# A chunked recurrence rebuilt as one fixed order of tasks, shorter placement lists, and 33 matmuls that nothing reads

## The chip, the cores and the metric

The kernel runs on one core of a Trainium2 chip. The metric is device time in microseconds (us) of one execution; three executions of the kernel before took 553.8, 552.11 and 552.08 us, the median being 552.11 us. The core has five engines with a queue of instructions each: TensorE (PE, whose weight loads are shown apart as PEld), VectorE (DVE), ScalarE (ACT), GpSimd (POOL) and SyncE (SP), which issues most of the DMA transfers. An engine carries out its own queue in order and waits on semaphores for what others make.

## The reference

Two parts follow one another. The first is a delta-rule recurrence over 768 time steps for 4 batches x 8 heads, with a 48x48 state each; the second sends each of the 3072 tokens (the 8 heads' outputs side by side, 384 numbers) to the best of 8 experts, a two-layer network with 1024 hidden units.

```python
k_n = k / (norm(k) + 1e-6)
for t in range(768):                         # state: 48 x 48 per batch and head
    y[t]  = q[t] @ state
    state = state + beta[t] * outer(k_n[t], v[t] - k_n[t] @ state)
x = y as 3072 rows of 384
logits = x @ w_gate + modality_bias[modality_id]
e = argmax(logits); gate = softmax(logits)[e]
out[tokens of e] = gate * (relu(x @ w1[e]) @ w2[e])
```

With this input only two experts are chosen, by 1508 and by 1564 tokens, so that the experts' work is five blocks ("slots") of 512 tokens, two of 256 and one of 128 in both kernels.

## The kernel before, in words

**Recurrence.** Time is cut into 12 chunks of 64 steps. A group step i = 2c+g (24 of them) treats chunk c for half of the 32 sequences. For each half step `gram` (L124) multiplies the keys with keys and queries: per sequence pair one stationary tile KB of 112x128, in which the keys of two sequences stand block-diagonally. KB is filled by copies (L111 to L113, the helper's L32 and L33) for each half step. The product gives the key Gram matrix and, beside it, the query-key matrix, which is masked to its lower triangle (L143 on DVE for the late half, on POOL in L145 for the early one).

From the Gram matrices come inverses of 32x32 triangular blocks. They are made for six sets m = 0..5, one after another, by `inverse_`: 30 pairs of a multiply (L213) and a subtract (L214), each pair for one column, on 128 partitions; rows 0 to 12 of each set go to DVE (tiles `tm_x`), the rest to POOL (`tm_y`). Set 0 is made in blocks of 16 which matmuls (L247, L253) join. `level` puts the blocks together to 64x64 for a group step (L326, a scaled copy `ys`, L335, a copy of R, and the scaling of the values in L340 on POOL).

`chain_` is the sequential part, one call per group step, each of which needs the state left by the step of the same g before it: L363 (ks, keys times state), a subtraction on DVE (L365, RHS), L378 (z, the inverse applied), a copy by ACT (ZT), L386 (state update into PSUM tile Sps), L372 and L394 (the output y), copies of the state (Sbd) and the output (xo), and a store of xo to DRAM (xd) by SP. `route` turns the outputs (L463) and multiplies them with the gate weights (L468, 128x96 wide).

**Routing.** `rank` finds each token's expert and its rank there. `lists` turns ranks into lists "place to token": for 6 tiles of 128 tokens at a time DVE makes a one-hot tile `l0` (L508) and two tiles `l1` with NH columns per token tile (L562 to L564), and PE multiplies them (L566). `part_a` treats the first 18 token tiles (four slots a0..a3 come from it), with NH = 16; `part_b` all 24 (slot b0, two of 256 and one of 128, and what is only needed by other inputs), with NH = 44.

**Experts.** Slots follow one another in the order a0, a1, a2, a3, b0, c0, c1, e0. A slot loads its expert's weights, gathers its tokens from xd (POOL), turns them (L659), splits weights (L674 high part on ACT; low part L675 on DVE, and on POOL for a1 and b0) and tokens (L661, L662) into high and low halves, and multiplies three times for each product: layer 1 in L690, followed by relu (L692, L693), layer 2 in L733, scaled by the gate (L736) and scattered to the output (L737). Slots of 128 tokens use L710.

**What sets the order.** The tile framework decides the order of each engine's queue from the program's order, priorities and a model of durations; the program sets a few priorities itself (`part_b` is under a raised one) and ties some instructions behind others. `tile_kernel` (L740) calls `gram`, `inverse`, `chain`, `route` and `level` in a loop (L777) and then runs the slots.

Of the kernel before, what the change touches and what calls it, by code (L numbers as in the profile page):

```python
# [14 lines left out]
class C:  # L15
    fl=4; mw=1; wn=2; kqb=5; kbb=2; thr=9; g0=17; nh=4; LA=2; LA0=1; ge=14; ge1=16; lgk={0:11,1:15,2:17,3:17}; gg={(12,0):('jy',0),(12,1):('jr',0),(13,0):('y1',0),(13,1):('r',0)}; ga=1; i1l=1; gdq=1;  gw=0; ww=512; t2e='vector'; dq1=('scalar','scalar'); jn={1:((1,0),)}; pf=0; gs=0
    invat={3:0,7:1,11:2,15:3,19:4,23:5}
    pgk=12; pgb=2; pgr=3; pg_q='sync'; gdb=2; kqr=2; kvb=2; r64=2; rtb=1; rcb=3; rbb=1; abuf=2; xob=2
    kb_q='sync'; gdfix='vector'; gdv=4; tmem='vector'; ascale='vector'; rscale='vector'; rcopy='mask'; rm_e='gpsimd'; vq='gpsimd'; yev='scalar'; sv=()
    x_q='sync'; xa_q='sync'; kv_q='sync'; ld_q='sync'; inv_q='sync'; w_q='sync'  # L20
    ap=(0,1); rp=(0,1); ra={0:('scalar','vector'),1:('scalar','vector')}; rs=(0,); i0=16; kb1=('scalar','vector'); g1=1; yq=2; na=1; xgb=4; wlp=('a1','b0'); wlq=(0,1,2,3); hpa=0; hpb=1; wide=1; zte=('scalar','scalar'); zti=4; pC_=None; pcn=(); gpt=('mo','ks','mo','y'); gpn=16; wte='vector'; ls=0; sp1=12; ti='gpsimd'; gde='scalar'; gde0='vector'; e16='scalar'; rh0='scalar'; as0='gpsimd'; dq=('vector','vector'); k1=1; rtg='gp'; rl=-1; fk=0; fz=0; fy=0; fi=0
    cA=9; tB=22; gt_e='gpsimd'; lb_e='vector'; TA=512; SB=1; SC=2; SE=1; eo=0; hold=1
    A1=2; A2=4; A3=1; B1=6; B2=6; B3=1
    lg0=1; hs=12; hn=10; tmb=2
    split=range(6); sp=3; spe=1
    invp=(); kbc=24; dkb=0
    la_e='vector'; rw=dict(reuse_waits='tile'); pC=0; pI=None; pL=None; pin=(0,); pln=(0,); kbp=4; kbe0=('scalar','scalar'); kbe=('vector','vector'); pml=range(0,16); sp0=1; r0=6; NR=10; kg=0; a0=1; wr=4; gl=16; SA=4; i1=60

NS=16; NE=8
# [5 lines left out]
def ring(pool,k,name,dt=F32):  # L35
    return pool.tile([128,1536],dt,name=name,tag=f"ring{k}")

class Attention:
    """Chunked delta rule. Group step i=2c+g: 64 tokens of chunk c of batches 2g+p, heads 4h+j; x=4p+j."""
    def __init__(s,ident,ctx,pctx,tc,kq,kv,bblk,mask,xd,pm):  # L40
        nc=s.nc=tc.nc; s.tc=tc; s.kq,s.kv,s.bblk,s.xd,s.pm=kq,kv,bblk,xd,pm
        s.ident=ident; s.late=[]
        for n in ("PG","KE","KQ","KV","Pt","GU","GD","gd","D","RD","RE","R","W","GW","AW","Y1","IL","RR","RL","RW","LD","rr","todo","KD","PI"): setattr(s,n,{})
        pc=s.pc=ctx.enter_context(tc.tile_pool(name="ac",bufs=1))
        s.pl=ctx.enter_context(tc.tile_pool(name="al",bufs=2))
        s.pw=ctx.enter_context(tc.tile_pool(name="aw",bufs=2))
# [12 lines left out]
    def rings(s):
        nc=s.nc; ring=s.ring; V=nc.vector; pc=s.pc  # L60
        s.Ic=pc.tile([128,1,16],F32,name="Ic"); s.m16=pc.tile([128,1],F32,name="m16")
        V.tensor_reduce(s.Ic[:,0],s.ident.rearrange("p (q r) -> p r q",q=4)[:,0:16],AX.X,ALU.add)
        V.tensor_reduce(s.m16,s.Ic[:,0],AX.X,ALU.add)
        V.tensor_scalar(s.m16,s.m16,-1.0,None,ALU.add)
        s.RHS=ring("RHS",2,[128,8,96],nc.gpsimd)
        s.R64=ring("R64",C.r64,[128,16,64],nc.gpsimd)
        s.RTB=ring("RTB",C.rtb,[128,16,64],nc.gpsimd)
        s.ZT=ring("ZT",2,[128,8,96],nc.gpsimd)
        s.Sbd=ring("Sbd",2,[112,8,96],nc.gpsimd)
    def banks(s,router):  # L70
        nc=s.nc; s.router=router
        bank=[s.ps.tile([128,512],F32,name=f"Sps{g}",tag=f"S{g}") for g in range(2)]
        for t in bank: nc.vector.memset(t,0.0)
        s.Sps=[t[0:112,0:384].rearrange("r (j c) -> r j c",j=4) for t in bank]
        router.lg=[t[:,384:480].rearrange("r (c e) -> r c e",e=8) for t in bank]

    def early(s,ctx):
        nc,tc=s.nc,s.tc
        s.pe=ctx[0].enter_context(s.tc.tile_pool(name="ag",bufs=1))
        s.pi=ctx[1].enter_context(s.tc.tile_pool(name="ai",bufs=1,side="right"))  # L80
        wt=s.wt=s.pe.tile([128,512],F32,name="wt")
        getattr(nc,C.wte).memset(wt,0.0)
        wz=s.pm.tile([128,512],F32,name="wz",tag="mo",bufs=2)
        for r in range(C.wn): nc.tensor.matmul(wz[:,0:C.ww],wt[:,0:128],wt[:,0:C.ww],start=True,stop=True)
        s.KB=[s.pe.tile([112,8,128],F32,name=f"KB{g}") for g in range(C.kbb)]
        for g,t in enumerate(s.KB): (s.nc.vector,s.nc.gpsimd)[g%2].memset(t,0.0)

    def gate(s,ins): return s.tc.issue_after(ins.ins) if ins is not None else contextlib.nullcontext()

    def fetch(s,i):  # L90
        c,g=divmod(i,2)
        if c<2:
            if g==0: s.KQ[c]=s.pl.tile([112,2,8,2,64],F32,name=f"kqr{c}",tag="kqr",bufs=C.kqr)
            s.KE[i]=k=s.KQ[c][:,g]
        else: s.KE[i]=k=s.pe.tile([112,8,2,64],F32,name=f"ke{i}",tag="ke",bufs=C.kqb)
        w=None
        if c>=2: w=s.LD[C.kg] if i>=C.g0 and C.kg>=0 else s.GW.get(c-C.thr)
        with s.gate(w): s.KD[i]=getattr(s.nc,C.ld_q).dma_start(k,s.kq[c].rearrange("r (g x a t) -> r g x a t",g=2,x=8,a=2)[:,g])

    def gram(s,i):  # L100
        nc,tc=s.nc,s.tc; E=lambda n:getattr(nc,n)
        c,g=divmod(i,2); m,n=divmod(i,4)
        if g==0:
            s.PG[c]=ring(s.pr,c%C.NR,f"PG{c}")
            if m not in C.ap: s.gd[c]=s.pe.tile([128,2,2,4,32],F32,name=f"gd{c}",tag="gd",bufs=C.gdb)
        if n==0:
# [4 lines left out]
        for h in range(2):  # L111
            b=64*h
# [746 lines left out]
```

## Time and profile before

| | us |
|---|---|
| median of three runs | 552.11 |
| span of the profiled execution | 550.4 |
| start of the first expert matmul (L690, slot a0) | 295.64 |
| start of the first L690 of slot a1 | 352.87 |
| end of the last L733 | 540.05 |

The profile is of one execution. Its page gives busy time per engine, the span in slices, the DMA queues, a chain of waits followed back from the last instruction, and the costliest groups of instructions. In a row of a group, "L213 DVE TENSOR_TENSOR tm_x<-T,A 128x108 ... x165 | 57.8, 352 | 5.4 <-DVE PG L143 0.7" stands for: line 213 on DVE, tile tm_x made from T and A, 165 instructions, 57.8 us busy in total and 352 ns in the mean, and 5.4 us idle ahead of them, most of which ended when the named instruction did. A row of a timeline has the start, the busy time, and the instruction, with "x16" for 16 like records in a row (one fp32 matmul leaves two records). A table by stretches has for each engine the busy time and the number of records, then PEclk, the TensorE clock that was granted as a share of full speed, the busy share of the DMA engines and their GB/s. A busy TensorE at a low granted clock does less work in the same time.

### The profile page before, as it was taken

How to read it: one execution, taken by the hardware profiler on the slowest of the kernel's cores; microseconds unless marked ns; L12 is line 12 of the kernel's file. 1: busy time of each engine (PE TensorE's matmuls, PEld its weight loads, DVE VectorE, ACT ScalarE, POOL GpSimd, SP SyncE). 2: the span in 40 equal slices, each digit the busy share in tenths (PEclk: the TensorE clock that was granted, in tenths of full speed). 3: DMA queues.
4: the chain of work that ended last, by engine and by line, in shares of the span. 5: the costliest groups of instructions: out<-in, count | busy, mean ns of one | idle time of the engine just before them, and what ended most of it. 6: DMA issues, size and time to landing. Idle time of an engine off the chain costs nothing. (4 is left out here: it accounts for less than half of the span.)

```text
span 550.4 us, 14025 instructions
## 1 busy us (share of the span) xinstructions
PE 483.5 (88%) x5459; PEld 432.1 (79%) x5459; DVE 364.5 (66%) x877; ACT 263.5 (48%) x619; POOL 208.5 (38%) x350
## 2 busy tenths in 40 slices
PE   7876875897898897998889997799999999999992
PEld 5776865786687776787768896689889898899992
DVE  5999899998789689577474499435536233437850
ACT  6855631655766567476565403043424334216540
POOL 9863477065066263111142136242303437111110
PEclk9977796588899799798889998699999999999997
DMA  8979741233594975838864224233623524427720
GB/s 205 247 200 238 176 105 55 64 95 89 169 226 138 236 180 166 209 120 230 228 192 142 76 80 127 75 116 114 209 79 120 170 75 164 128 78 227 233 85 9
DMA packets 82716, 80.81 MB, mean 147 GB/s; under 512 B 50105, under 2 KB 73671, under 8 KB 81520
## 3 DMA queue, kind: packets, MB, share of 16 engines
q1 hardware_dynamic: 79440, 70.18, 46.8%
q0 software_dynamic: 3200, 9.64, 5.2%
q8 instruction: 45, 0.74, 0.6%
q14 instruction: 31, 0.25, 0.2%
HBM read 65.12 MB, written 14.88 MB: 145 GB/s over the span
## 5 line engine op out<-in xcount | busy, mean ns | idle before, releaser
L733 PE MATMUL opa<-w2ha,h 128*128 128x384 f32 x256 | 69.1, 339 | 0.3 <-DVE ooa L736 0.3
L213 DVE TENSOR_TENSOR tm_x<-T,A 128x108 f32<-128x108 f32 (+12 forms) x165 | 57.8, 352 | 5.4 <-DVE PG L143 0.7
L124 PE MATMUL gp<-ke,KB 112*128 112x128 f32 x320 | 53.1, 331 | 9.3 <-DVE PG L143 3.9
L214 DVE TENSOR_TENSOR T<-T,tm_x 128x108 f32<-128x108 f32 (+12 forms) x165 | 56.8, 346 | 4.5
L124 PEld LDWEIGHTS gp<-ke,KB 112*128 112x128 f32 x320 | 48.3, 238 | 12.3 <-issue 3.7
L693 DVE SCALAR_TENSOR_TENSOR h<-hpa,h 128x512 fp32r<-128x512 f32 x32 | 22.0, 689 | 42.4 <-ACT h L692 42.4
L733 PEld LDWEIGHTS opa<-w2ha,h 128*128 128x128 f32 x256 | 46.2, 188 | 1.4 <-DVE ooa L736 0.5
L733 PE MATMUL opa<-w2la,h 128*128 128x384 f32 x128 | 43.0, 336 | 0.0
L692 ACT ACTIVATE h<-hpa 128x512 fp32r<-128x512 f32 x32 | 19.1, 596 | 49.5 <-PE hpa L690 49.5
L690 PE MATMUL hpa<-x,w1ha 128*128 128x512 f32 x144 | 39.1, 408 | 0.0
L340 POOL TENSOR_TENSOR kvn<-kvn,RR 128x384 f32<-128x384 f32 x22 | 18.7, 868 | 50.7 <-DMA kvn<-in_kv_dram 28.3
L363 PE MATMUL ks<-Sbd,kqr 112*64 112x96 f32 x352 | 27.3, 274 | 8.7 <-DMA kqr<-in_kq_dram 4.8
L365 DVE TENSOR_TENSOR RHS<-kvn,ks 64x384 f32<-64x384 f32 x44 | 24.2, 551 | 15.8 <-POOL kvn L340 9.4
L214 POOL TENSOR_TENSOR T<-T,tm_y 128x18 f32<-128x18 f32 (+8 forms) x90 | 30.7, 342 | 6.6
L213 POOL TENSOR_TENSOR tm_y<-T,A 128x18 f32<-128x18 f32 (+8 forms) x90 | 30.5, 339 | 6.6
L690 PEld LDWEIGHTS hpa<-x,w1ha 128*128 128x128 f32 x144 | 27.3, 194 | 5.5
L32 ACT COPY ZT<-z 64x384 f32<-64x384 f32 x48 | 22.7, 473 | 17.2 <-PE z L378 16.6
L363 PEld LDWEIGHTS ks<-Sbd,kqr 112*64 112x64 f32 x352 | 20.9, 150 | 11.8 <-ACT Sbd L32 4.4
L32 ACT COPY Sbd<-Sps 48x192 f32<-48x192 f32 x88 | 27.5, 313 | 5.2 <-PE Sps L386 2.7
L737 POOL DMA_INDIRECT out_dram<-ooa,sidxa x16 | 17.1, 1071 | 32.6 <-DMA out_dram<-ooa,sidxa 13.1
L657 POOL DMA_INDIRECT xga<-xd,gidxa x16 | 17.9, 1117 | 30.5 <-PE xpa L659 17.4
L378 PE MATMUL z<-RHS,R 128*64 128x96 f32 x384 | 26.9, 296 | 1.6 <-ACT R L338 1.6
(346 smaller groups left out, 1173.7 us busy)
## 6 DMA issues: line engine op xcount, KB each, us to landing
kvn<-in_kv_dram SPq DMA_DIRECT2D x12, 768.0 KB, 8.0
ke<-in_kq_dram SPq DMA_DIRECT2D x20, 448.0 KB, 6.8
kqr<-in_kq_dram SPq DMA_DIRECT2D x10, 896.0 KB, 6.9
w1ra<-in_moe_w_dram SPq DMA_DIRECT2D x16, 384.0 KB, 4.0
w2ra<-in_moe_w_dram SPq DMA_DIRECT2D x16, 384.0 KB, 3.2
xd<-xo SPq DMA_DIRECT2D x24, 192.0 KB, 2.5
w1rc<-in_moe_w_dram SPq DMA_DIRECT2D x8, 384.0 KB, 3.6
w2rc<-in_moe_w_dram SPq DMA_DIRECT2D x8, 384.0 KB, 3.2
```

Of the source, the lines that this page charges most:

```text
L32: if n=="scalar": nc.scalar.copy(o,i)
L124: nc.tensor.matmul(gp[p][:,j,:],KB[:,x,:],k[:,x].rearrange("r a t -> r (a t)"),start=True,stop=True)
L213: yield I.tensor_tensor(o,y,z,ALU.mult)
L214: yield I.tensor_tensor(x,x,o,ALU.subtract)
L340: if c: E(C.vq).tensor_tensor(V,V,w,ALU.mult)
L363: nc.tensor.matmul(ks[64*p:64*p+64,:,j,:],KQ[:,4*p+j,0],hc(Sb[:,4*p+j,:]),start=True,stop=True)
L365: b=64*p; nc.vector.tensor_tensor(RH[b:b+64,:,48*p:48*p+48].rearrange("q (h j) c -> q h j c",h=2),VN[b:b+64],ks[b:b+64],ALU.subtract)
L378: s.PI['z',i]=nc.tensor.matmul(z[64*h:64*h+64,:,j,:],R[:,2*j+h,:],hc(RH[:,4*h+j,:]),start=True,stop=True)
L690: nc.tensor.matmul(hp[:,v,:],w[:,k,fs],x[:,k,0:T],start=(n==0),stop=(n==8)); n+=1
L692: nc.scalar.activation(hh,hp,AF.Relu)
L693: nc.vector.scalar_tensor_tensor(hl,hp,0.0,hh.bitcast(F32),ALU.max,ALU.subtract)
L733: mm=nc.tensor.matmul(op,h[:,f%nf,ts_],w[:,f%2,:],start=(n==0),stop=(n==23)); n+=1
```

## The change

The recurrence is written as about 916 named tasks (load, gram, copy, one pair of an inverse, one product of a step, ...), each with the tasks that it needs. A string of their numbers, `ORDER`, gives the one order in which they are emitted; a letter behind a number puts the task on another engine than its usual one (d DVE, a ACT, g POOL). `in_order` then chains the instructions of each engine, so that they keep this order. Also new:

- Gram matrices without KB: for each chunk 32 matmuls of 64x64 for keys with keys and, as a task of its own, 32 for queries with keys. The copies into KB go, and the mask is always applied by DVE.
- Inverses for two sets in one instruction, JOBS = ((0,1),(2,3),(4,5)): sets 0 and 1 as 16-blocks with joins on the chip, the others with two sets side by side. 27 of 60 pairs of these stand on POOL, the rest on DVE.
- Gate logits for four token tiles together (12 matmuls of 32x128 instead of 3 of 128x96 for each tile).
- The routing of the first 16 token tiles (8 columns, two slots a0, a1), and slot a0's loads, gathers, token turning and its first four of eight layer-1 parts are tasks in the same order; the slots are now a0, a1, b0, b1, b2, c0, c1, e0.
- `part_b` makes 17 columns instead of 44, for 4 tiles at a time; the remaining 35 are made only in the branch for other inputs, which this input does not take in either kernel.
- Ten matmuls of the identity at the start (`WARM`) in place of two of 512 columns, and 33 of them at 16 places of the order (`FILL`) into a part of a PSUM tile that nothing reads.
- All low halves of weights are made on DVE (`wlp` is empty).

```diff
+JOBS=((0,1),(2,3),(4,5)); SPL=(0, 32, 32)
+NS=16; NE=8; NC=24; WARM=10
+ORDER="""\
+167 42 2 0 26 54 161 58 56 43 55 57 65 44d 46d 59 47a 68d 66 27 69a 162 36 67 75 45 53 48 76 28 70 159 79 3 64 80 1 77 29 163 78 81 86 4 87 160 164 165 88 89 90 49 337 166 30 338
...
+FILL="""\
+444:3 82:1 150:6 857:2 382:1 869:1 725:1 492:3 867:1 806:1 632:2 511:4 521:1 554:2 357:3 559:1"""
...
+    def order(s):
+        out=[]; done=set()
+        for n in ORDER.split():
+            t=s.T[int(n.rstrip("dag"))]; out.append(t)
+            if n[-1] in "dag": t["eng"]=dict(d="DVE",a="ACT",g="POOL")[n[-1]]; assert t["eng"] in t["alt"]
...
+def in_order(tc,first):
+    last={}
+    for i in tc.nc.cur_bb.bb.instructions[first:]:
+        e=i.engine
...
+        if e in last: tc.add_manual_dep(i,last[e].name,mybir.DependencyInfo(mybir.DependencyClass.NoSync,mybir.DependencyReason.DATA),reason="order")
+        last[e]=i
...
-                nc.tensor.matmul(gp[p][:,j,:],KB[:,x,:],k[:,x].rearrange("r a t -> r (a t)"),start=True,stop=True)
+            for g in range(2):
+                for j in range(4):
+                    for p in range(2):
+                        for h in range(2):
+                            u=64*(h^p); x=4*p+j; l=s.KQ[c][u:u+48,g,x,0] if a else s.KE[c][u:u+48,g,x]
+                            s.I[f"g{c}"]=mm(t[p][64*h:64*h+64,64*(4*g+j):64*(4*g+j)+64],l,s.KQ[c][u:u+48,g,x,1] if a else l,start=True,stop=True)
...
+                    E[s.e].tensor_tensor(o,T[:,:,lo:lo+na,c:c+1].to_broadcast([128,n,na,nb]),X[:,:,c:c+1,c+1:32].to_broadcast([128,n,na,nb]),ALU.mult)
+                    x=T[:,:,lo:lo+na,c+1:32]; E[s.e].tensor_tensor(x,x,o,ALU.subtract)
...
+                add(f"rl{i}","SP",2.4,lambda i=i: rld(i),[f"rd{J}",f"re{J}",f"z{i-4}",f"y1_{i-2}"],mb=.75); need=[f"rl{i}"]
...
+            add(f"z{i}","PE",.73,lambda i=i: z(i),[f"rh0_{i}",f"rh1_{i}",f"rc{i}",old("zt0_{}",i,1),old("zt1_{}",i,1),"r1_1"],prio=top)
+            for h in range(2): add(f"zt{h}_{i}","ACT",.5,lambda i=i,h=h: zt(i,h),[f"z{i}",old("pz{}",i,2),old("ds{}",i,2)],prio=top,alt=dict(ACT=(.48,0),DVE=(.56,0)))
...
+            for n,m in fill.get(t["k"],()):
+                with s.tc.issue_after(s.I[m].ins) if m else contextlib.nullcontext():
+                    for _ in range(n): s.nc.tensor.matmul(s.S[1][:,384:512],s.ident,s.ident,start=2 not in s.gp,stop=True,skip_group_check=True)
+            s.e=t["eng"]; t["fn"]()
+        return in_order(s.tc,first)
...
+        def lg():
+            s.lg[u]=A.mo(f"lg{u}")[:,0:128]
+            for k in range(3):
+                for j in range(4): nc.tensor.matmul(s.lg[u][32*j:32*j+32],s.wg[:,k],A.xs[4*u+j][:,k],start=(k==0),stop=(k==2))
...
-        s.lists("b",24,pi,4*C.SB+2*NS+NE,out,pw,ps,tag,0)
+        yield from s.lists("b",24,pi,s.nm,s.ids[:,0:s.nm],0,out,pw,bank("tpb")[:,0:2*s.nm].rearrange("q (a b) -> q a b",a=2),6,False)
```

The first place where rows move is TensorE's queue around one group step in the middle of the recurrence. Before (z is L378, state update L386, output L394 and L372, level L326 and L335, gate logits L468, turned outputs L463):

```order
L378 MATMUL z_2988<-RHS_339,R_342 64x2x48 x8
L468 MATMUL Sps_408<-wg,rxs_2931 128x96 x3
L326 MATMUL y_2946<-RTB_346,PG_508 32x64 x8
L386 MATMUL Sps_409<-ZT_349,kvn_2501 48x96 x8
L394 MATMUL y_3007<-ZT_349,PG_457 64x2x48 x8
L335 MATMUL y_2946<-R_343,ys_2955 32x32 x16
L363 MATMUL ks_3182<-Sbd_353,kqr_2936 64x2x48 x8
L372 MATMUL y_3101<-Sbd_352,kqr_2936 64x2x48 x8
L463 MATMUL rxt_3031<-ident,xo_3028 128x128 x3
```

After, the same products have other lines (z L422, ks L416, state update L428, output L439 and L436, level L380 and L388, turned outputs L569), and L498 is a filler:

```order
L422 MATMUL z_3384<-RHS_151,R_141 64x2x48 x8
L569 MATMUL rxt_3393<-ident,xo_3201 128x128 x3
L416 MATMUL ks_3409<-Sb_158,kqr_129 64x2x48 x8
L428 MATMUL S<-ZT_155,kk_3025 48x96 x8
L436 MATMUL y_3429<-Sb_159,kqr_130 64x2x48 x8
L380 MATMUL lv_3439<-RTB_144,gk_716 32x64 x8
L498 MATMUL S<-ident 128x128
L439 MATMUL y_3429<-ZT_155,pb_3243 64x2x48 x8
L569 MATMUL rxt_3462<-ident,xo_3418 128x128 x3
L388 MATMUL lv_3439<-R_140,ys_3459 32x32 x16
```

The logits no longer stand between z and the state update, the next step's ks comes ahead of the state update, and a filler stands in the step.

The second place is DVE's queue within an inverse. Before, one set's pairs with few elements, and the next set's first pairs among them:

```order
L213 TENSOR_TENSOR tm_x_1292<-T_1133,A_1132 128x24
L214 TENSOR_TENSOR T_1133<-T_1133,tm_x_1292 128x12x2
L213 TENSOR_TENSOR tm_x_1295<-T_1133,A_1132 128x12
L213 TENSOR_TENSOR tm_x_2036<-T_2015,A_2014 128x30
L214 TENSOR_TENSOR T_1133<-T_1133,tm_x_1295 128x12
L214 TENSOR_TENSOR T_2015<-T_2015,tm_x_2036 128x30
```

After, two sets in one instruction (128x2x30), with the subtractions of the chain (L418, formerly L365) and a copy of z (L26) between them:

```order
L418 TENSOR_TENSOR RHS_151<-vv_1517,ks_1902 64x8x48 x2
L26 COPY ZT_155<-z_2028 64x8x48
L334 TENSOR_TENSOR tmx_1_2073<-T_2000,A_1755 128x2x30
L335 TENSOR_TENSOR T_2000<-T_2000,tmx_1_2073 128x2x30
L418 TENSOR_TENSOR RHS_150<-vv_1724,ks_2040 64x8x48 x2
L334 TENSOR_TENSOR tmx_3_2101<-T_2000,A_1755 128x2x84
L335 TENSOR_TENSOR T_2000<-T_2000,tmx_3_2101 128x2x3x28
```

A copy that ACT made before stands in DVE's queue here, and a pair without its number in the row (column 2) stands on POOL.

The third place is TensorE's queue where the second lists are made. Before, between slot a0's last product and slot a1's first (L690), beside a1's tokens (L659):

```order
L659 MATMUL xpa_0_5041<-ident,xga_0_5039 128x128 x3
L566 MATMUL tpb<-l1b,l0b 128x88 x12
L659 MATMUL xpa_1_5049<-ident,xga_1_5047 128x128 x3
L659 MATMUL xpa_2_5057<-ident,xga_2_5055 128x128 x3
L659 MATMUL xpa_3_5065<-ident,xga_3_5063 128x128 x3
L566 MATMUL tpb<-l1b,l0b 128x88 x12
L690 MATMUL hpa_0_5083<-x_4701,w1ha_0_5071 128x512 x3
```

After, inside slot a0's own products (L836 is layer 1, L891 layer 2), in three pieces of which this is the first, with 34 columns instead of 88:

```order
L891 MATMUL opa_1_5275<-w2ha_0_5088,h_4551 128x384
L891 MATMUL opa_1_5275<-w2la_0_5089,h_4550 128x384
L697 MATMUL tpb<-l1b,l0b 128x34 x8
L836 MATMUL hpa_4_5120<-xh,w1xa_2_4938 128x512 x3
L836 MATMUL hpa_4_5120<-xl,w1xa_2_4938 128x512 x3
```

What stood in a gap between two slots now stands among matmuls of the first slot, which the lists do not need.

More of the change, by code (lines that the diff above doesn't have):

```diff
@@ new lines, in xp @@
+        def xp(t): x["p",t]=s.mo(f"xp_{t}")[:,0:384].rearrange("q (k t) -> q k t",k=3); s.X.turn(x["g",t],x["p",t])
+        for t in range(4):
+            add(f"xg{t}","POOL",1.1,lambda t=t: xg(t),["xe","xd15",end,f"xg{t-1}" if t else None],prio=900,mb=.25,port=0)
+            add(f"xp{t}","PE",.4,lambda t=t: xp(t),[f"xg{t}"],prio=900,take=dict(mo=1))
+            add(f"xh{t}","ACT",.5,lambda t=t: s.X.xhi(t,x["p",t]),[f"xp{t}"]+tfree,prio=900)
+            add(f"xl{t}","DVE",.57,lambda t=t: s.X.xlo(t,x["p",t]),[f"xh{t}"],prio=900,give=dict(mo=1))
```

1155 lines of the change are left out of this document (610 added, 545 removed).

## Prediction

> **What bounds the kernel now.** I read the table by stretches first, then the groups, the timeline at two seams, and the chain of waits at the end.
>
> ```profile
> span 550.4 us, 14025 instructions
> 0.00:295.60 295.60, 247.74 (x4142) 216.12 (x4142) 236.07 (x632) 176.04 (x482) 135.41 (x291) 0.86 0.66 171
> 40.00:80.00 40.00, 31.75 (x508) 28.58 (x506) 36.69 (x89) 20.22 (x70) 21.27 (x47) 0.83 0.78 189
> 80.00:120.00 40.00, 30.28 (x612) 26.84 (x612) 37.46 (x105) 18.15 (x52) 17.93 (x52) 0.66 0.19 52
> 120.00:160.00 40.00, 34.05 (x607) 28.96 (x607) 32.94 (x94) 25.75 (x67) 15.71 (x38) 0.91 0.57 158
> 320.00:360.00 40.00, 32.93 (x172) 30.77 (x171) 29.73 (x99) 7.08 (x11) 16.56 (x13) 0.83 0.29 89
> 360.00:400.00 40.00, 40.00 (x204) 35.83 (x203) 18.76 (x27) 15.19 (x24) 13.12 (x12) 1.00 0.51 157
> PE ks L363 <- DMA kqr<-in_kq_dram: 4.8, 3, 2.3
> ```
>
> The columns are the stretch, its length, busy PE, PEld, DVE, ACT and POOL, then granted clock, DMA share and GB/s. Up to 295.6 the recurrence has two near-bounds. DVE is 92 to 94% busy from 40 to 120 (36.69 and 37.46 of 40), where the inverses are made, and PE's clock there is 0.83 and 0.66; from 120 on PE is 85% busy at 0.91. From 360 on PE alone is the bound, at full clock. DMA shows 0.66 over the whole recurrence, and the longest of PE's sums of waits (last row: us, times, longest) is 4.8 for a load.
>
> ```profile
> 62.18 0.88 PE L378 MATMUL z<-RHS,R 128*64 128x96 f32 x16 [0.93 <-ACT R L338]
> 157.82 0.88 PE L378 MATMUL z<-RHS,R 128*64 128x96 f32 x16
> 164.63 0.88 PE L378 MATMUL z<-RHS,R 128*64 128x96 f32 x16
> 211.66 0.88 PE L378 MATMUL z<-RHS,R 128*64 128x96 f32 x16
> 295.64 1.67 PE L690 MATMUL hpa<-x,w1ha 128*128 128x512 f32 x6
> 300.40 0.88 PE L378 MATMUL z<-RHS,R 128*64 128x96 f32 x16
> 334.44 0.49 PE L659 MATMUL xpa<-ident,xga 128*128 128x128 f32 x3
> 337.79 3.92 PE L566 MATMUL tpb<-l1b,l0b 128*128 128x88 f32 x24 [2.87 <-DVE l1b L564]
> 344.88 0.55 PE L659 MATMUL xpa<-ident,xga 128*128 128x128 f32 x3 [1.91 <-DVE x L662]
> 347.73 5.42 PE L566 MATMUL tpb<-l1b,l0b 128*128 128x88 f32 x24 [2.29 <-DVE l1b L564]
> 352.87 2.91 PE L690 MATMUL hpa<-x,w1ha 128*128 128x512 f32 x6
> 540.05 0.03 issue
> ```
>
> The rows of z (L378) are steps of the recurrence: the first is at 62.18, and one step takes 6.8 us (157.82 to 164.63) where PE's own work fills it. The others cut the span: recurrence to 295.64, slot a0 to 334.44 (38.8), a hole in which PE waits for DVE's lists to 352.87 (18.4), the other slots to 540.05 (187.2), and a tail of 10.35 to 550.4. The span is 1.7 below the median of 552.11; I sum spans and add 1.7 at the end.
>
> **DVE in the recurrence.** It has 236.1 us of work in the first row above.
>
> ```profile
> L213 DVE TENSOR_TENSOR tm_x<-T,A 128x108 f32<-128x108 f32 (+12 forms) x165 | 57.8, 352 | 5.4 <-DVE PG L143 0.7
> L214 DVE TENSOR_TENSOR T<-T,tm_x 128x108 f32<-128x108 f32 (+12 forms) x165 | 56.8, 346 | 4.5
> L192 DVE TENSOR_TENSOR A<-A,t 128x1024 f32<-128x1024 f32 x5 | 6.1, 1218 | 0.0
> L213 DVE TENSOR_TENSOR tm_x<-T,A 128x228 f32<-128x228 f32 x5 | 2.5, 499 | 0.2
> L214 DVE TENSOR_TENSOR T<-T,tm_x 128x228 f32<-128x228 f32 x5 | 2.0, 398 | 0.2
> L33 DVE COPY KB<-ke 48x512 f32<-48x512 f32 x28 | 15.5, 553 | 0.8 <-PE gp L124 0.3
> L143 DVE TENSOR_TENSOR PG<-gp,um 128x256 f32<-128x256 f32 x16 | 6.6, 416 | 1.5 <-ACT gd L32 1.2
> L32 ACT COPY ZT<-z 64x384 f32<-64x384 f32 x48 | 22.7, 473 | 17.2 <-PE z L378 16.6
> L32 ACT COPY Sbd<-Sps 48x192 f32<-48x192 f32 x88 | 27.5, 313 | 5.2 <-PE Sps L386 2.7
> L330 ACT ACTIVATE ys<-y 32x256 f32<-32x256 f32 x48 | 18.0, 375 | 17.9 <-PE y L326 17.6
> L340 POOL TENSOR_TENSOR kvn<-kvn,RR 128x384 f32<-128x384 f32 x22 | 18.7, 868 | 50.7 <-DMA kvn<-in_kv_dram 28.3
> ```
>
> Gone: the 330 pairs' halves (57.8+56.8 = 114.6) and 15.5 of copies into KB, which leaves 106. Added are the new pairs, 96 instructions over 28,840 columns where the old 330 had 40,920. From 128x228 (398 ns) to 128x1024 (1218 ns) a column costs 1.03 ns beside some 160 ns for each instruction: 96x0.16+28.8x1.03 = 45. The mean of the old pairs is dearer (the same 228 columns take 499 ns in L213 than 398 in L214): 330x0.16 leaves 62 for 40.9 thousand columns, 1.5 ns each, which gives 59. I take 52 with 45 and 59 as bounds. The mask for all chunks is 48x0.416 = 20.0 instead of 6.6, so +13.3. Copies that the order gives to DVE, priced by ACT's rows: 21 of z x0.473, 30 of the state x0.313, 14 of ys x0.375 and 14 of 384 columns x0.48 are 31. Seven scalings of values from POOL: at a half to all of 0.868, 3 to 6. The joins of eight group steps (16 sums, 8 transposes, 4 scalings, smaller than 0.5 each) I estimate at 8. Sum 106+52+13+31+5+8 = 215, bounds 206 to 223. The routing and the splits before the first expert matmul are in both numbers.
>
> How long does 215 take? In 40 to 120 DVE kept 93%; in 120 to 160 82%. Its first work stands some 7 us into the span. 215 at 0.88 and 7 more is **251**; at 0.93 it is 238, at 0.80 276. I take the middle since copies of the chain now stand in DVE's queue and wait there for PE, with pairs of an inverse behind them that nothing else holds back.
>
> **PE in the recurrence.** 247.7 us busy at a clock of 0.86 are 213 at full clock, a high estimate, as waits within a busy stretch count too.
>
> ```profile
> 20.09 2.02 PE L124 MATMUL gp<-ke,KB 112*128 112x128 f32 x16 [1.11 <-ACT s L175]
> 161.80 0.69 PE L335 MATMUL y<-R,ys 32*32 32x32 f32 x32
> 159.77 0.64 PE L326 MATMUL y<-RTB,PG 128*32 128x64 f32 x16 [0.23 <-DMA RTB<-RE]
> 160.34 0.87 PE L386 MATMUL Sps<-ZT,kvn 128*48 128x96 f32 x16
> 165.44 0.91 PE L468 MATMUL Sps<-wg,rxs 128*128 128x96 f32 x6
> ```
>
> Grams: 24 half steps of 16 records at 2.02 are 48 before. After, 768 matmuls leave 1536 records of 64x64, a tile that no row shows. At the pace of L335's small tiles (0.69 for 32) they cost 33, at that of L326 with 64 columns (0.64 for 16) 61; four quadrants at once by that pace would be 15. I take 33, nearest in shape, so -15 with -33 and +13 as bounds. Logits: 24x0.91 = 22 before; after, 144 records of 32 columns' width, between a quarter and all of L468's 0.15 each for 4/3 of the columns: 7 to 29, I take 14, so -8. Fillers and warm-up, 43 matmuls of 128 columns by L468's 0.15 for each of two records: +13. That leaves 213-15-8+13 = 203, less the waits in the 213; I take 195. At a clock of 0.87 it is 224 of the 251, and so PE is late second. With grams and logits at their dear ends (61 and 29) PE has 238, which takes 274 and makes PE the bound: the whole then comes to 515.
>
> [...]
>
> **Fillers and clock.** Where the fillers stand in waits, they cost nothing; where PE is already late, they cost the 13 above, which I left in. I give the new stretch 0.87, the mean of before being 0.86, and count no gain for fillers. The row 80 to 120 shows what a better clock would be worth: 30.28 busy at 0.66 is 20 at full clock.
> [...]
>
> **Experts.**
>
> ```profile
> L675 DVE TENSOR_TENSOR w2la<-w2ra,w2ha 128x768 fp32r<-128x768 f32 x12 | 11.5, 956 | 3.0 <-ACT w2ha L674 2.5
> ```
>
> The slots' matmuls are the same in number. Slot a0 took 38.8 beside the recurrence's end; I give it 36. The lists of stage b go from 88 to 34 columns and stand among a0's products: 48 records by L566's 3.92 for 24 times 34/88 are 3.0, and 2 for waits. The other slots keep 187.2, as their first 18.4 hole is not part of it; the token turning of a1, four of 0.55, is +2 (hidden in the hole before). That the low halves of two slots' weights move from POOL to DVE is covered: DVE is 18.76 of 40 busy in 360 to 400; without that cover it were 16x0.956 us, 15 in all. Tail 10.35 stays, since the last slot is the same. Sum: 251+36+5+187.2+2-1+10.35 = 490.5, where -1 is the part of a0's first product that lies beside the recurrence's last output; with 1.7 around the span **492**.
>
> **Rivals.** Two rows of the list of transfers first:
>
> ```profile
> R<-RD SPq DMA_DIRECT2D x32, 64.0 KB, 7.1
> RTB<-RE SPq DMA_DIRECT2D x16, 64.0 KB, 5.4
> ```
>
> (1) *The fixed order stalls.* Every engine waits at the head of its queue, and what stands behind waits too: the nine old steps from 211.66 to 300.40 took 9.9 each. A likely head is SP: the loads of R and RTB (last numbers of their rows: us from issue to landing) wait for a level two steps earlier and stand behind stores. If all go at 9.9 from the first z at 62, the last z is at 289, the first expert matmul some 5 earlier as before (295.64 to 300.40), and the time 526; with half of that, 509. For it: nothing can be put past a late one any more. Against: queues were in order before as well, and PE and DVE have 10% of slack. (2) *DVE's load falls to its low end and its share is that of 40 to 120:* 206/0.93+7 = 229, so 470, where PE's 195 keeps up only at a clock of 0.9 or more (217). (3) *Slower:* the clock stays low wherever inverses are made, as in 80 to 120 (0.66), now that two sets at a time go through one engine for the whole recurrence. 195 us of PE work at 0.55 take 355, and the time is 596; it decides from 0.62 down, where 195/0.62 = 315 gives 556. Against: from 120 on the clock was 0.91 with DVE at 82%, and the steps now begin earlier, so PE isn't left to DVE alone. (4) *The change doesn't do what it says:* inverses in pairs of sets make each set's result later, so the chain starts late and gains nothing: recurrence as before, only the hole goes: 552.1-18.4+5+2 = 541.
>
> **How the numbers follow.** Forecast 0.66, with 480 to 510 as its own range; rival 1 0.14, rival 2 0.09, rival 4 0.06, slower 0.05. The range of 8 in 10 reaches from 466 (below rival 2) to 528 (rival 1), which leaves out rival 4, slower and the edges. A measurement can tell 0.3%, or 1.7 us, from no change. Faster 0.93, within 0.3% 0.02 (the end of rival 4), slower 0.05.
>
> **What would show it.** Right: the first expert matmul near 250; DVE busy near 215 up to it with a share of 0.85 to 0.93; no hole over 3 us around the second lists; the slots after a0 in 187 to 190. Wrong: DVE share under 0.8 with waits for DMA or PE at its head (rival 1), clock under 0.7 in the windows to 200 (slower), the first z later than 90 (rival 4).

## The result, and the profile after

The changed kernel took 512.53 us (median of four runs, 509.33 to 514.34), the kernel before 552.1 beside it; the ratio is 0.929, with a 95% interval of 0.923 to 0.934. The forecast was 492 with a range of 466 to 528. The profiled run took 509.33, of which the span is 507.5. Ratios, their intervals and the differences taken below leave out executions more than 1.5% above the fastest of the same kernel, one of which (e9_beforefill) took 880.94.

First the table by stretches of the changed kernel, with the columns of the one before: from the start to the first expert matmul, the part of it behind the first z, and the stretch from 40 to 80.

```profile
0.00:265.15 265.15, 226.23 (x5398) 200.41 (x5399) 200.04 (x459) 135.92 (x345) 88.38 (x136) 0.85 0.67 156
70.40:265.15 194.75, 173.72 (x4221) 151.19 (x4220) 147.30 (x342) 102.88 (x260) 64.09 (x79) 0.95 0.67 162
40.00:80.00 40.00, 37.10 (x712) 35.51 (x708) 31.87 (x71) 22.00 (x65) 14.16 (x22) 0.50 0.38 94
```

The recurrence ends at 265.15 instead of 295.64. Behind the first z TensorE is now the busier engine: 89% at a clock of 0.95, DVE 76%. But the start has grown worse: from 40 to 80 TensorE is busy 93% at a granted clock of 0.50.

The seams in TensorE's timeline of the same kernel:

```profile
70.44 1.55 PE L422 MATMUL z<-RHS,R 128*64 128x96 f32 x16
257.50 0.83 PE L422 MATMUL z<-RHS,R 128*64 128x96 f32 x16
265.15 0.94 PE L836 MATMUL hp<-xh,w1xa 128*128 128x512 f32 x3
314.62 1.87 PE L697 MATMUL tpb<-l1b,l0b 128*128 128x34 f32 x16
322.54 1.87 PE L697 MATMUL tpb<-l1b,l0b 128*128 128x34 f32 x16
329.58 1.87 PE L697 MATMUL tpb<-l1b,l0b 128*128 128x34 f32 x16
```

And the end of its chain of waits (start, us, what):

```profile
492.12 4.34 PE ope L891 x23
497.64 0.71 POOL out_dram L895
```

The first z comes at 70.44, 8.3 later than before. From there to the first expert matmul it is 194.7 instead of 233.5, so 38.8 less. The experts take 507.5-265.15 = 242.35 instead of 254.8, so 12.4 less: no hole stands around the lists any more. 8.3 lost, 38.8 and 12.4 won make the 42.9 between the two spans. The lists (L697) stand among slot a1's products: the first slot's last layer-2 product ends before 305.4, and a1's first L836 is at 295.5. The text on the change and the prediction put them into slot a0; slot b0 is the first that needs them.

DVE's groups up to 265.15 in the changed kernel (busy, mean ns of one, idle time ahead):

```profile
L418 DVE TENSOR_TENSOR RHS<-vv,ks 64x384 f32<-64x384 f32 x44 | 24.3, 552 | 4.1 <-PE ks L416 1.9 <-POOL vv L393 1.0
L334 DVE TENSOR_TENSOR tmx<-T,A 128x440 f32<-128x440 f32 (+14 forms) x33 | 17.5, 532 | 2.7 <-POOL T L335 1.4 <-POOL T L260 0.5
L335 DVE TENSOR_TENSOR T<-T,tmx 128x440 f32<-128x440 f32 (+14 forms) x33 | 17.5, 530 | 1.2
L26 DVE COPY ZT<-z 64x384 f32<-64x384 f32 x21 | 11.6, 554 | 12.1 <-PE z L422 7.6 <-ACT ZT L25 4.3
L272 DVE TENSOR_TENSOR T<-T,tm 128x60 f32<-128x60 f32 (+7 forms) x15 | 5.2, 350 | 0.5
L271 DVE TENSOR_TENSOR tm<-T,A 128x60 f32<-128x60 f32 (+7 forms) x15 | 5.2, 348 | 0.5
```

The 96 instructions of the pairs take 17.5+17.5+5.2+5.2 = 45.4, where the old 330 took 114.6. The most idle time in these groups, 12.1 us, stands before the copies of z, 7.6 of it until TensorE's z ends.

### The profile page after: what moved, and what is told of

It reads as the page before. It is cut to its first block, busy times and chain, and to the rows that moved or that the text cites. A ratio compares the mean times of both kernels' runs of the same rounds, so it can differ in the third digit from the quotient of the medians.

```text
span 507.5 us, 16007 instructions
## 1 busy us (share of the span) xinstructions
PE 455.3 (90%) x6685; PEld 409.9 (81%) x6685; DVE 333.7 (66%) x724; ACT 222.8 (44%) x480; POOL 134.6 (27%) x181
## 5 line engine op out<-in xcount | busy, mean ns | idle before, releaser
L891 PE MATMUL opb<-w2hb,h 128*128 128x384 f32 x192 | 52.9, 341 | 0.5 <-DVE oob L894 0.5
L836 PE MATMUL hpb<-xh,w1xb 128*128 128x512 f32 x144 | 40.9, 395 | 0.0
L891 PEld LDWEIGHTS opb<-w2hb,h 128*128 128x128 f32 x192 | 34.8, 188 | 1.8 <-DVE oob L894 1.0
L891 PE MATMUL opa<-w2ha,h 128*128 128x384 f32 x128 | 34.6, 341 | 0.0
L334 POOL TENSOR_TENSOR tmx<-T,A 128x168 f32<-128x168 f32 (+13 forms) x27 | 20.3, 752 | 48.7 <-DVE T L335 47.3
L891 PE MATMUL opb<-w2lb,h 128*128 128x384 f32 x96 | 32.5, 338 | 0.0
L836 PEld LDWEIGHTS hpb<-xh,w1xb 128*128 128x128 f32 x144 | 26.7, 188 | 4.6
L25 ACT COPY Sb<-S 48x192 f32<-48x192 f32 x58 | 18.1, 313 | 21.6 <-PE S L428 10.2
L418 DVE TENSOR_TENSOR RHS<-vv,ks 64x384 f32<-64x384 f32 x44 | 24.3, 552 | 4.1 <-PE ks L416 1.9
L891 PEld LDWEIGHTS opa<-w2ha,h 128*128 128x128 f32 x128 | 23.2, 188 | 0.8
L335 POOL TENSOR_TENSOR T<-T,tmx 128x168 f32<-128x168 f32 (+13 forms) x27 | 22.2, 821 | 2.1
L25 ACT COPY ZT<-z 64x384 f32<-64x384 f32 x27 | 12.8, 472 | 22.1 <-DVE ZT L26 12.1
```

The costliest lines, as they stand in the source:

```text
L25: if n=="scalar": nc.scalar.copy(o,i)
L334: E[s.e].tensor_tensor(o,T[:,:,lo:lo+na,c:c+1].to_broadcast([128,n,na,nb]),X[:,:,c:c+1,c+1:32].to_broadcast([128,n,na,nb]),ALU.mult)
L335: x=T[:,:,lo:lo+na,c+1:32]; E[s.e].tensor_tensor(x,x,o,ALU.subtract)
L418: c,g=divmod(i,2); b=64*p; V.tensor_tensor(s.RHS[g][b:b+64,:,48*p:48*p+48].rearrange("q (h j) c -> q h j c",h=2),s.KV[c,1][b:b+64,g],s.ks[ ...
L836: if n in ks: mm=s.nc.tensor.matmul(hp[:,v,:],w[:,k,fs],x[:,k,0:T],start=(n==0),stop=(n==8))
L891: mm=nc.tensor.matmul(op,h[:,f%nf,ts_],w[:,f%2,:],start=(n==0),stop=(n==23)); n+=1
```

## Experiments

Twelve kernels ran, in three groups; within a group they shared a chip with the kernel before. The medians of the kernel before were 549.97, 551.91 and 547.69. Differences against the changed kernel are taken from all eight of its runs, first and repeated, 509.3 to 519.7, unless another is named.

**What lowers the clock.** A block of streams stands ahead of everything else:

```diff
             t=s.bank("warm","z")
-            for _ in range(WARM): mm(t[:,0:128],s.ident,s.ident,start=True,stop=True)
+            full(40); join(14,16); gram(14); join(14,16); lv(16); join(14,16); z(14); join(14,16); join(14,32); join(10,16,1); join(14,16); join(10,16,2)
```

> The changed kernel with a block of TensorE streams ahead of everything else, on the identity, read by nothing: 128x128 matmuls, then streams without gaps of the joins' 64x64 tiles with 16 columns, of the grams' 64x64 tiles, of the level's 32x32 tiles, of z's 128x64 tiles with 96 columns, and joins with one or two 128x128 matmuls in each 16. Theory A (a queue full of small tiles lets the granted clock fall, gaps or not): clock 0.5 during the streams of joins and 1.0 in those of z and of 128x128, although PE is busy all the time in each. Theory B (only idle stretches lower the clock): 1.0 in every stream after the first. The time is that of the changed kernel and of the streams, 620 to 760 us, and is not compared.

It took 765.43 us, streams included. The table by stretches of this kernel, one stretch within each stream: 128x128, joins, level tiles (32x32), z (128x64), joins of 16 and 32 columns, and joins with one and with two 128x128 in each 16:

```profile
2.00:13.00 11.00, 11.00 (x79) 11.00 (x80) 0.97 (x2) 0.30 (x2) 10.75 (x24) 1.00 0.81 176
19.00:34.00 15.00, 15.00 (x285) 15.00 (x286) 0.00 (x0) 0.00 (x0) 0.00 (x0) 0.50 0.18 54
81.00:94.00 13.00, 13.00 (x496) 13.00 (x494) 0.00 (x0) 0.00 (x0) 0.00 (x0) 0.50 0.02 5
119.00:129.50 10.50, 10.50 (x214) 10.50 (x212) 0.00 (x0) 0.00 (x0) 0.00 (x0) 0.82 0.01 3
130.00:176.00 46.00, 46.00 (x912) 46.00 (x912) 0.00 (x0) 0.00 (x0) 0.00 (x0) 0.53 0.01 2
177.00:200.00 23.00, 23.00 (x311) 20.60 (x309) 0.00 (x0) 0.00 (x0) 0.00 (x0) 0.50 0.00 1
226.50:254.00 27.50, 27.50 (x328) 25.14 (x328) 0.00 (x0) 0.00 (x0) 0.00 (x0) 0.50 0.01 2
```

Theory A holds: in 46 us of joins without any idle time, with 16 and then with 32 columns, the mean clock is 0.53 (0.50 from 135 on), while the stream of z tiles brought it up: 0.82 in the mean, 0.50 until 121, 1.00 from 123 on. Two 128x128 among 16 joins did not bring it up (0.50 from 226.5 to 254). So joins alone can hold the clock at 0.50, as between 40 and 80 in the changed kernel, where they stand. It had fallen there ahead of them: it is 0.50 from 10 on, among grams with waits between them. (The stream of grams, which also had waits, has 0.62 and 0.75 in two stretches.)

**More fillers there.** 46 more of them, as many as two ahead of each join:

```diff
 FILL="""\
-... 511:4 521:1 554:2 357:3 559:1"""
+... 511:4 521:1 554:2 357:3 559:1 123:10 192:6 200:2 202:2 208:2 210:2 216:2 218:2 224:2 226:2 232:2 234:2 240:2 242:2 248:2 250:2 194:2"""
```

> The changed kernel with 46 more fillers ahead of the first chain step: ten before the last early gram, where TensorE waits for a load, six before the first join and two before each other join. Theory A (fillers in number bring the clock up in the stretch from 40 to 80): clock above 0.9 there, first z at 58 to 64 instead of 70.4, time -4 to -10 us. Theory B (two 128x128 among 16 small tiles do not raise it, as in the streams): clock 0.5 to 0.65 there, fillers cost up to 14 us in a stretch where TensorE is busy anyway, first z at 72 to 84, time +2 to +12 us.

Four runs took 514.24, 527.42, 521.08 and 534.65, a median of 524.25. The same fillers ran once more in a kernel told of below (e12_both). The stretch from 40 to 80 in the profiled run of the first, which took 514.24:

```profile
40.00:80.00 40.00, 36.87 (x811) 33.12 (x804) 32.71 (x74) 24.80 (x72) 15.72 (x24) 0.92 0.35 91
```

The same stretch in the profiled run of the other, which took 537.4:

```profile
40.00:80.00 40.00, 38.73 (x514) 34.95 (x503) 23.70 (x55) 15.35 (x44) 10.20 (x18) 0.55 0.37 92
```

One join and its two fillers in the timeline of the first:

```profile
44.35 1.12 PE L295 MATMUL jo<-w1b,gk 64*64 64x32 f32 x32
45.40 0.71 PE L498 MATMUL S<-ident 128*128 128x128 f32 x4
```

And in that of the other:

```profile
44.94 1.92 PE L295 MATMUL jo<-w1b,gk 64*64 64x32 f32 x32
46.79 1.22 PE L498 MATMUL S<-ident 128*128 128x128 f32 x4
```

In both runs the clock had come up by the first join: it was 0.50 from 20 to 30, 64 gram records took 2.46 ahead of the ten fillers and 1.17 and 1.45 behind them, and the first join took 1.12. In the first run the mix kept it (1.00 from 40 to 70). In the second it fell at the fillers behind that first join (they took 0.95), and the mix did not raise it again in the 40 us that follow (0.50 from 50 to 90). TensorE had waited 0.88 ahead of the first join in the one and 1.27 in the other; whether that is the reason isn't shown. The first z came at 67.0 in the one and at 84.9 in the other. Each theory has its clock in one run. But Theory A has neither its first z (58 to 64) nor its gain: 514.24 is no faster than the 514.1 that the eight runs of the changed kernel have as their median. The two clocks fit the scatter: of the eight runs of both kernels, two have a mean granted clock of 0.941 and 0.944 and took 514.24 and 510.42; the others have 0.889 to 0.919 and took 521.08 to 537.4. (That something else disturbed the run of 537.4 as well isn't excluded; that such a mix stayed at 0.50, the streams show by themselves.) Where the first z came 3.4 early, the first expert matmul stood at 265.36 all the same (265.15 without): the lead was lost on the way.

**Without fillers.**

```diff
-FILL="""\
-444:3 82:1 150:6 857:2 382:1 869:1 725:1 492:3 867:1 806:1 632:2 511:4 521:1 554:2 357:3 559:1"""
+FILL=""
```

> The changed kernel without the 33 fillers; the ten matmuls at the start stay. Theory A (fillers hold the clock up): the clock between 82 and 265 us falls from 0.95 to under 0.90 and the time rises by 5 to 20 us, to 517 to 532. Theory B (fillers stand in waits and hold nothing): clock 0.93 to 0.96 there, and the time is that of the changed kernel within 3 us (509 to 515).

522.03 us (519.47 to 528.17), ratio 0.955 (0.946 to 0.965). Two stretches of this kernel:

```profile
70.00:100.00 30.00, 25.13 (x549) 22.95 (x548) 24.39 (x48) 17.06 (x49) 15.98 (x18) 0.65 0.39 90
100.00:140.00 40.00, 35.38 (x896) 30.86 (x896) 29.20 (x67) 24.84 (x62) 20.00 (x29) 0.87 0.68 176
```

The same two of the changed kernel:

```profile
70.00:100.00 30.00, 26.66 (x596) 23.79 (x596) 25.50 (x52) 17.73 (x51) 15.58 (x18) 0.81 0.39 90
100.00:140.00 40.00, 36.83 (x992) 31.52 (x988) 31.07 (x68) 25.92 (x65) 20.60 (x29) 1.00 0.71 189
```

The stretch from 82 to 265 in this kernel, in the changed one, and in the repeated run of the changed one (below):

```profile
82.00:265.00 183.00, 159.17 (x3915) 138.81 (x3911) 133.67 (x315) 92.76 (x232) 58.18 (x73) 0.93 0.72 171
82.00:265.00 183.00, 162.93 (x4008) 141.43 (x4009) 136.91 (x321) 96.02 (x239) 58.57 (x73) 0.98 0.72 172
82.00:265.00 183.00, 166.55 (x3954) 145.18 (x3952) 131.05 (x312) 91.44 (x229) 57.44 (x72) 0.93 0.70 163
```

The clock is lower where the fillers stood (0.65 and 0.87 instead of 0.81 and 1.00). But over the whole stretch it is 0.93, as in the repeated run, which has its fillers. So the time lies in Theory A's range and the clock in Theory B's. By the medians the kernel is some 7 us slower (521.2 against 514.1 of the eight runs); the interval of its ratio lies apart from the first measurement's and overlaps the repeated run's, so the size is not sharp.

Nor is the clock shown to be what costs the time. The last step's z begins at 259.65 instead of 257.50, 2.1 later; yet the first expert matmul is at 271.05 instead of 265.15, and the span is 10.2 longer. What comes between stands in ACT's queue. Here three casts of weights, the first waiting for its load, come ahead of the copy of the last z, and TensorE's output product waits 4.96 for that copy:

```profile
263.98 0.83 ACT L822 CAST w1xa<-w1ra 128x768 fp32r<-128x768 f32 x1 [4.40 <-DMA w1ra<-in_moe_w_dram]
266.93 0.47 ACT L25 COPY ZT<-z 64x384 f32<-64x384 f32 x1
267.45 1.55 PE L438 MATMUL y<-ZT,pb 128*64 128x96 f32 x16 [4.96 <-ACT ZT L25]
```

In the changed kernel the copy comes ahead of the casts:

```profile
259.94 0.47 ACT L25 COPY ZT<-z 64x384 f32<-64x384 f32 x1 [2.51 <-DVE ZT L26]
262.24 0.83 ACT L823 CAST w1xa<-w1ra 128x768 fp32r<-128x768 f32 x1 [1.32 <-DMA w1ra<-in_moe_w_dram]
```

Another 4.3 are lost in the experts, at a wait told of under the lists. So 2.1 of the 10.2 stand in the recurrence up to its last step; the rest goes with ACT's queue, which came out otherwise, and with that wait. What the fillers have to do with either isn't shown, nor what they are worth by the clock beyond the 2.1.

**The order.** The chain of `in_order` was taken from all engines, from all but TensorE, and from TensorE alone:

```diff
-        if e in last: tc.add_manual_dep(i,last[e].name,...
+        if 0: tc.add_manual_dep(i,last[e].name,...                                   # e5_noorder
+        if e in last and e==mybir.EngineType.PE: tc.add_manual_dep(i,last[e].name,...   # e10_peorder
+        if e in last and e!=mybir.EngineType.PE: tc.add_manual_dep(i,last[e].name,...   # e11_nope
```

> The changed kernel with the same tasks emitted in the same sequence, but without the chain that fixes each engine's order, so that the framework's scheduler sorts the queues again. Theory A (the fixed order carries the gain of the recurrence): first expert matmul later than 280 us, time 525 to 550. Theory B (the rebuilt tasks carry it): within 6 us of the changed kernel, 506 to 518.

> The changed kernel with the fixed order on TensorE's queue alone; the scheduler sorts the others. Theory A (TensorE's order carries what the order gives): 508 to 525 us. Theory B (the order of DVE and ACT carries it, since their queues decide when TensorE's operands come): 560 to 610 us, near the 606.7 without any fixed order.

> The changed kernel with the fixed order on every engine but TensorE, whose queue the scheduler sorts. Theory A (the order of DVE, ACT and the DMA queue carries what the order gives, as the run with TensorE's order alone at 613 us suggests): 510 to 535 us. Theory B (it takes all engines' orders together; one queue sorted by another model spoils the rest): over 560 us.

They took 606.72 (ratio 1.106, 1.099 to 1.113), 613.26 (1.105, 1.100 to 1.109) and 515.73 us (0.943, 0.934 to 0.952), the last beside 516.53 of the changed kernel in the same group. The first lies far beyond Theory A's range, the second just above Theory B's, the third in Theory A's. The stretch from 40 to 200 without any fixed order:

```profile
40.00:200.00 160.00, 108.20 (x2131) 96.64 (x2125) 92.67 (x197) 60.40 (x162) 56.86 (x75) 0.65 0.34 80
```

With TensorE's alone:

```profile
40.00:200.00 160.00, 101.27 (x2083) 91.20 (x2080) 91.69 (x195) 59.32 (x160) 57.30 (x75) 0.65 0.35 80
```

With all but TensorE's:

```profile
40.00:200.00 160.00, 145.70 (x3276) 130.20 (x3274) 117.68 (x246) 87.14 (x227) 62.49 (x84) 0.82 0.62 148
```

And in the changed kernel:

```profile
40.00:200.00 160.00, 143.65 (x3438) 128.37 (x3432) 123.58 (x257) 89.44 (x233) 64.35 (x86) 0.85 0.63 155
```

The rebuilt tasks without their order are slower than the kernel before by a tenth. What carries the gain is the order of the queues besides TensorE's: with it, TensorE's own may be left to the scheduler, whose queue then differs from the fixed one in places only. Without it DVE is 58% busy instead of 77% and TensorE has a clock of 0.65. Which of the other queues it is (DVE, ACT, POOL or SP's transfers) was not taken apart.

**The lists.** The columns were taken back to 44 in the changed kernel, and cut to 17 in the kernel before, where their place stays between slots a0 and a1 (the last slot's column moves with them; columns for other inputs are left out there):

```diff
-        n=4*C.SB+2*C.SC; m=4*C.SB+2*NS; s.nm=n+C.SE; s.ids=...
+        n=4*C.SB+2*C.SC; m=4*C.SB+2*NS; s.nm=44; s.ids=...
```

```diff
-        s.lists("b",24,pi,4*C.SB+2*NS+NE,out,pw,ps,tag,0)
+        s.lists("b",24,pi,17,[o[:,0:17] for o in out],pw,ps,tag,0,ids)
```

> The changed kernel with 44 columns in the second lists instead of 17. Theory A (the number of columns closed the hole): PE +2.2 us for 88 instead of 34 columns and DVE some 6 us more in the first slot, and a hole of several us opens there: +6 to +12 us. Theory B (the place among the first slot's products closed it): DVE has room, only PE's own 2 us show: +1 to +3 us.

> The kernel before with 17 columns in the second lists (its own place for them unchanged). Theory A (size makes the hole): the hole of 18.4 us between slots a0 and a1 shrinks to under 11 and the time falls by 5 to 9 us. Theory B (the place makes it: PE waits for DVE's chain of small instructions between two slots whatever the size): the hole stays at 14 or more, time -1 to -4 us.

521.37 us (515.78 to 523.62) for the first, ratio 0.947 (0.938 to 0.956); 547.5 for the second beside 551.91, ratio 0.991 (0.988 to 0.995). The recurrence of the first differs from run to run, so its experts are read alone, in its profiled run of 523.62: from its first L836 at 273.53 to its end at 521.9 they take 248.4, where the changed kernel takes 242.35 and its repetition 242.0. TensorE's products with 88 columns in the timeline of the first kernel:

```profile
323.34 1.91 PE L697 MATMUL tpb<-l1b,l0b 128*128 128x88 f32 x16
```

Its one wait of size by TensorE's table of waits behind 273 (us in total, times, longest):

```profile
PE hpb L836 <- ACT xh L801: 4.1, 1, 4.1
```

And the hole in the timeline of the kernel before with 17 columns:

```profile
333.07 0.49 PE L660 MATMUL xpa<-ident,xga 128*128 128x128 f32 x3
335.59 4.00 PE L566 MATMUL tpb<-l1b,l0b 128*128 128x34 f32 x24 [2.03 <-DVE l1b L564]
348.15 2.79 PE L691 MATMUL hpa<-x,w1ha 128*128 128x512 f32 x6
```

The first is some 7 us slower than the changed kernel, in Theory A's range; the second's hole is in Theory B's, and its time just past it. On TensorE the columns cost nothing: 1.91 with 88 against 1.87 with 34 for 16 records, and in the kernel before 4.00 with 34 against 3.92 with 88 for 24. With 44 columns the experts take 6 us more, and slot b0 waits 4.1 for its tokens. But the wait isn't shown to come from the columns. With 17 columns it stands at slot b0 too, in the profiled runs without fillers and with more fillers:

```profile
PE xpb L798 <- DVE xl L801: 4.4, 1, 4.4
PE xpb L799 <- DVE xl L802: 4.3, 1, 4.3
```

Their experts take 246.7 and 247.1. And with 44 columns the first gather for b0 starts 68.4 after the first L836, in the changed kernel 67.6, so that the lists are done only 0.8 later. The columns are worth between 1 and 6 us there, by this one profile. In the kernel before the fewer columns win 4.4, but the hole stays at 15.1 (333.07 to 348.15) of 18.4. So the smaller part of the 12.4 goes to the size; the larger goes to the place and to what else changed in the experts, which was not taken apart.

**Fillers in the kernel before.** Two 128x128 in each step's z bank, placed by the scheduler:

```diff
-... fk=0; fz=0; fy=0; fi=0
+... fk=0; fz=2; fy=0; fi=0
```

> The kernel before with two 128x128 fillers in each step's z bank, 48 in all, placed by the framework's scheduler. Theory A (the low clock of 80 to 120 comes from small tiles and gaps and costs time): clock there above 0.8, time -3 to -12 us. Theory B (DVE holds that stretch): clock up or not, time within 3 us or up to +12 us, as the fillers cost 0.6 us in each step that TensorE bounds.

551.67 beside 551.91, ratio 0.999 (0.996 to 1.001). The stretch of 80 to 120:

```profile
80.00:120.00 40.00, 30.27 (x577) 26.76 (x576) 37.33 (x106) 16.98 (x49) 17.58 (x52) 0.59 0.16 47
```

The clock did not rise there (0.59, and 0.66 before), and only 4 of the 96 records of the fillers stand in that stretch, so this run does not tell what a better clock would be worth there. Theory B's time came out, without its reason being shown.

**The repeated run, and the third inverse.** The gaps of the changed kernel at 184 and 191 stand where the third pair of sets comes back from DRAM. Its last pairs were moved from POOL to DVE (e7_dve2), and the same with the early fillers (e12_both):

```diff
-... 323g ... 324g ... 325g ... 326g ... 327g ... 329g
+... 323 ... 324 ... 325 ... 326 ... 327 ... 329
```

> The changed kernel again, unchanged, beside the next three on one chip. Both theories of those: 509 to 515 us, ratio 0.925 to 0.935.

> The changed kernel with the last pairs of the third inverse (columns 24 to 28 and 30) on DVE instead of POOL. Theory A (between 175 and 195 the recurrence waits for the third inverse's way through DRAM, which starts when its last pair ends at 174.6): pairs end some 3 us earlier, TensorE's gaps at 184 and 191 shrink from 4.8 together to under 3, time -1 to -5 us. Theory B (the gaps are the DMA queues' own, busy 0.95 there, or the added pairs hold up the chain's copies on DVE): -1 to +4 us.

> The changed kernel with the 46 early fillers of before and the last pairs of the third inverse on DVE. Theory A (an earlier first step is worth something once the third inverse comes earlier): time -4 to -9 us against the changed kernel beside it. Theory B (another wait follows): within 4 us of it.

The repeated kernel took 516.53 (512.52 to 519.65), ratio 0.947 (0.937 to 0.958); with the moved pairs 511.16 (507.44 to 514.7), ratio 0.936 (0.925 to 0.947); with both 528.1 (510.42 to 537.4). In this group the kernel before itself took 541.98 to 552.81, and all its comparisons, that without TensorE's order among them, are unclear. The first two intervals overlap, so whether the moved pairs help isn't told. Nor is the reason confirmed: the pairs ended at 182.0 with, and at 181.8 without. In both runs they were late already, for another reason, which TensorE's timelines show, the repeated run's (two rows) and that with the moved pairs (one):

```profile
128.90 0.59 PE L436 MATMUL y<-Sb,kqr 112*64 112x96 f32 x3 [3.08 <-issue]
137.71 1.99 PE L180 MATMUL gp<-kqr 48*64 48x64 f32 x64
126.91 0.38 PE L436 MATMUL y<-Sb,kqr 112*64 112x96 f32 x3 [2.81 <-issue]
```

The same place in the first profile of the same kernel:

```profile
126.81 0.38 PE L436 MATMUL y<-Sb,kqr 112*64 112x96 f32 x3 [0.34 <-issue]
```

In the repeated run TensorE stood still for 3.08 us, waiting for nothing that the profile shows, and then worked at half clock (0.50 from 130 to 140; 64 gram records took 1.99, against 1.16 at full clock) until 141. From the z ahead of it to the next one it was 20.4 us (124.41 to 144.82), in the first profile 12.9 (125.06 to 137.95): 7.5 us lost at one place, of which 6.8 are left at the first expert matmul (271.93). The run with the moved pairs lost 5.8 there (122.70 to 141.42) after its 2.81, and that with 44 columns 5.1 (125.35 to 143.31) after a pause of 1.99 at the same instruction. What the pause is, is open. That it costs two to three times its length (7.5 for 3.08, 5.8 for 2.81, 5.1 for 1.99) is read from these three runs; that the half clock behind it is the reason, from the repeated run, and was not tried by itself.

## Why the prediction was right in kind, and 20 us too low

- **Recurrence.** 251 forecast, 265.15 measured. The failed step is "215 at 0.88": DVE was to bound the recurrence. Its load is 200.0, below my bounds of 206 to 223, and its share 0.75. The pairs alone explain 7 of it (45.4 instead of 52: the lower bound, the dearer columns of the old pairs didn't come back). DVE had room. TensorE, which was to be late second with 224 busy of 251, was busy 226.2 of 265.15. So its busy time came as forecast; what came dearer is the time that it stood idle, 38.9 us (17.9 up to the first z, 21.0 behind it), where the forecast left it 27.
- **TensorE's 195** was near: 226.23 busy at 0.85 are 192. In it grams were near (24 groups of 64 records at 1.16 are 28 where I took 33; the bound of 15, four quadrants at once, was my supposition, and no run shows it), and logits below my lowest bound, 6x0.86 = 5 (bounds 7 to 29). At a change of tile shape the view shows no gap: 48x64 grams start at 132.43, before the 128x48 state update ahead of them ends (131.63 and 0.87). The 0.87 of the clock was right as a mean (0.85) and wrong as a picture: 0.57 up to the first z and 0.95 behind. The first z came at 70.4 instead of 62.2, with TensorE, not DVE, the busier one from 50 to 70 (19.43 and 15.91 of 20 us). That this stretch makes the error isn't shown: with more fillers the first z came at 67.0, and the first expert matmul no earlier.
- **Fillers.** "Count no gain" was an estimate and stays open: without them the time is some 7 us longer, but of the 10.2 in the profiled run only 2.1 stand in the recurrence up to its last step.
- **Experts.** 239.55 forecast, 242.35 measured. The hole went. The lists' price went wrong by "times 34/88": the columns don't price them, 48 records took 3x1.87 = 5.6 instead of 3.0. The tail was 11.05 instead of 10.35.
- **Around the span** 1.7 was right for the profiled run (509.33 to 507.5); the median lay 3 us above that run.
- **Rivals.** Rival 1 (stalls) came at most in part: each of the 23 steps from 70.4 to 257.5 took 8.1 us, where the mean before was 10.4 and the steady step 6.8, and TensorE stood idle 21.0 us in that part. A stall of its kind does show without fillers, where ACT's copy of z stands behind casts that wait for a load. Rival 3's cause, a low clock, did come, from 10 to 80 (0.50), where grams and joins stand, without its extent. Rival 4 is not what happened, but e5_noorder shows that the rebuilt tasks, in the scheduler's own order, would have been slower than the kernel before. I had no rival for that.
- The sum: +14.2 for the recurrence, +2.8 for the experts and 3.2 between the profiled run and the median are 20.2 of the 20.5 between 492 and 512.5; the rest is rounding and what lies around the span.

## What to carry to other kernels

Read the granted clock beside the busy share of the stretch: 32 records of a join took 1.92 at 0.50 and 1.12 at 1.00, and 46 us of joins without any idle time had 0.53, so here small tiles could be the whole reason. When work is rebuilt as tasks, its order on the engines that feed TensorE may be worth more than the tasks: measure the tasks without the order before praising them. A list, a copy or a gather goes beside products that don't need it; making it smaller alone left most of the hole (15.1 of 18.4). And where a run without some part is slower, look for the place before crediting the part: without fillers 8 of the 10 us stood elsewhere than in the steps that the fillers were to speed up.

## What the runs showed of the hardware that was not expected

- TensorE without idle time stayed at half clock for 41 us of 64x64 tiles with 16 and 32 columns (0.50 from 135 to 176, 0.53 from 130 on), and for 13 us of 32x32 tiles (0.50); in a stream of 128x64 tiles with 96 columns it was 0.50 until 121 and 1.00 from 123 on (0.82 from 119 to 129.5).
- The same queue of 32 small records and four of 128x128 held the full clock in one run (1.00; 1.12 and 0.71 us) and half of it in another (0.50; 1.92 and 1.22), for over 25 us each. The other run had begun the mix at full clock (1.12 for the first 32 records) and lost it.
- A product's time didn't follow its columns between 34 and 88: 1.87 and 1.91 us for 16 records.
- The granted clock of one profile didn't fit its times. In the profile with 44 columns it is 1.00 from 40 to 80, but 32 records of a join take 1.92, as they do at 0.50 elsewhere; its mean is 0.956 at 523.62 us, where the other three runs of that kernel have 0.896 to 0.899 at 515.78 to 522.4. Read the clock beside the durations.
